# A fused attention and two-layer expert kernel: the first sequence's heads in two parts, and a separate buffer in the weight decode

## The chip, the cores and the metric

The kernel runs on one core of one Trainium2 chip. The metric is the device time of one execution in microseconds (us). Before the change the median of three runs is 915.22 us (913.24 to 915.87). The profiled execution, on which all sums below are made, took 915.09 us.

## What is computed

Three layers follow one another on 2304 tokens (4 sequences of 576, 8 heads of 64, so 512 features). The first is an attention that adds a coarse one over groups of four tokens and a local one over the neighbours less than four tokens away:

```python
q_d = q.reshape(B, H, Sd, factor, D).mean(axis=3)      # the same for k and v; factor = 4, Sd = 144
out_up = np.repeat(sm_attn(q_d, k_d, v_d), factor, axis=2)
mask = np.abs(pos[:, None] - pos[None, :]) < factor
...
attn = np.exp(scores)                                  # scores outside the mask are -1e9
out_local = np.matmul(attn, v)
return out_up + out_local
```

The second is a gated layer, `silu(x @ w_gate) * (x @ w_val) @ w_out`, with 512 x 1536 and 1536 x 512 weights. The third routes each token to one of eight experts (cosine similarity with an embedding) and returns `gate * (relu(x @ w1[e]) @ w2[e])`.

## The kernel before

**The order of the work.** Nothing in this kernel is written in the order in which the engines run it. Every piece of work is a generator; a small planner (`Sched`) keeps a free time for each engine, takes the waiting piece with the lowest priority number that is ready, and emits its instruction. What it costs each operation at stands in the `yield op("ACT", t_act(512))` lines and in the functions `t_dve`, `t_act`, `t_pool`, `t_dma`; buffers are handed out by class (`w`, `ps`, `raw`, ...), and a piece can wait for an event (`yield ("wait", ...)`). The result is one fixed list of instructions for each engine, and each engine then runs its own list strictly in order, so an instruction that waits holds up all behind it.

**Attention.** A pair of heads fills the 128 partitions; there are 16 pairs, four for each sequence. For a pair, `heads` loads q and k (transposed, features on partitions), v for the local part and v for the coarse one into a set of five buffers. `local` cuts the 576 queries into ten units of 58 (64 rows, 64 keys each). In the first sequence it does for a pair: scores on TensorE (L584, 20 small matmuls), the mask added on VectorE while it copies the scores from PSUM (L590, two operations), maximum, subtraction (L594, L596), exponential on ScalarE (L598), sum, reciprocal, product on GpSimd (L606). `local_piece` transposes the weights (L624, 5 transposes of 128 x 128), multiplies with v (L642) and adds the coarse part into the tokens' tile (L649). `down` is the coarse part: sums of four queries and of four keys on VectorE (L498), scores on TensorE (L508, 4 matmuls), exponentials (L524), product (L533), transposes (L541), and the product with v (L558). For the first four pairs (`NV = 4`) v isn't summed over its groups first: TensorE accumulates over the four tokens of a group in 16 matmuls.

**Chunks.** The tokens are then taken in nine chunks of 256 (`CT`). Chunk 0 holds tokens 0 to 255 of the first sequence, chunk 1 tokens 256 to 511, chunk 2 starts with its last 64. `x_split` and `x_piece` split a chunk's 128-feature block k (which is pair k of the sequence) into a rounded part `xhi` (L694, ScalarE) and the rest `xlo` (L697, VectorE for even k, GpSimd for odd); a product then takes three matmuls.

**The gated layer.** `gated` goes over the six 256-wide blocks p of the hidden features, chunks 0 and 1 in turn for each p, and later chunk after chunk. `gemm1` multiplies (L740): for each half j of the block, first all four k of the gate weights, then all four k of the value weights, into one PSUM bank. `act_h` applies the gate, and `gemm2` multiplies with `w_out` (L772). The first `gemm1` needs all four pairs of the first sequence.

**The weights** of this layer come as 64-bit words and are turned into float32 on the chip, in tiles of 128 x 512 (`decode`, 36 of them): VectorE shifts the low words in place (L343), ScalarE scales the high words in place (L346) and then writes a 16-bit number into the upper half of each low word (L350), VectorE joins the two (L353), ScalarE rounds (L358), GpSimd forms the rest (L360). The places that L346 reads and writes lie 8 bytes apart, and so do those that L350 writes.

**Until the first chunk's first block is there**, `keep_warm` fills TensorE's list with matmuls on zeros (L318, 128 x 512, bfloat16): while the event `("x", 0, 0)` isn't set in the plan, one is put wherever the plan has TensorE free. They are fixed entries of the list and run whatever the other engines do.

Of the kernel before, what the change touches and what calls it, by code (L numbers as in the profile page):

```python
# [30 lines left out]
E = 8  # L31
# [22 lines left out]
NCST = P + NPAIR * WK + 3 * E + 4 * NT18 + NOV  # L54
# [151 lines left out]
TOKENS = {'dq': 4, 'raw': 6, 'scatter': 1, 'pat': 4, 'pm': 1, 'early': 4, 'late': 1}  # L206
# [4 lines left out]
NV = 4  # L211
WEIGHT_P = [1.0, 2.0, 3.0, 4.0, 4.5, 4.8]


def build(tc, a):
# [64 lines left out]
    nc.gpsimd.memset(tinit, OOB)  # L280
    nc.scalar.dma_start(out=tab.rearrange("(p n) o -> p (n o)", p=P), in_=tinit)
    def small_consts():
        yield ("lag", 20000)
# [5 lines left out]
        nc.scalar.copy(ones, t01[:, P:2 * P])  # L289
        sc.put("w", t01)  # L290
# [9 lines left out]
    slots("t2", gm, 2, [P, DM])  # L300
# [25 lines left out]
    def decode(cls, src, dst, nm, p, j):  # L326

        yield ("get", "dq")
        raw = yield ("get", cls)
        if j == 1:  # L330
            sc.set((nm, p, "t"))
        r = raw[:, 0:1024].bitcast(I32)
        yield dma(P * 4096)
# [53 lines left out]
    def prep_en():  # L387
        t = yield ("get", "t2")
        t1 = yield ("get", "t2")
        en, junk = t[:E, :], t1[:E, :]  # L390
# [13 lines left out]
        ps = yield ("get", "ps")  # L404
# [6 lines left out]
        sc.put("t2", t)  # L411
        sc.put("t2", t1)
# [28 lines left out]
    def heads(n):  # L441
# [51 lines left out]
    def down(n, sq, sk, sd):  # L493
# [52 lines left out]
        if n < NV:  # L546
            parts = [sd[:GH, 256 * x + D * i:256 * x + D * (i + 1)] for x in range(4) for i in range(4)]
        else:
            parts = [vd_of(sk)[:, x, :] for x in range(4)]
            yield ("wait", ("vfree", n))  # L550
# [9 lines left out]
        if n < NV:  # L560
            sc.set(("vfree", n))
# [7 lines left out]
    def local(n, sq, sk, sv, sa, st):  # L569
# [41 lines left out]
        sc.set(("done", n))  # L611

# [629 lines left out]
    with tc.manual_schedule():  # L1242
# [9 lines left out]
        sc.spawn(6, prep_en(), 0.0)  # L1252
# [64 lines left out]

def consts():
# [55 lines left out]
```

## Time and profile before

| | before |
|---|---|
| three runs, median (lowest to highest) | 915.22 us (913.24 to 915.87) |
| the profiled execution: its time / its span | 915.09 us / 913.3 us |
| TensorE busy, share of the span | 886.4 us, 97% |
| VectorE / ScalarE / GpSimd busy | 443.7 / 395.4 / 287.9 us |
| moved by DMA | 87.99 MB, mean 96 GB/s |

The span runs from the first to the last instruction on the core; 1.8 us of the execution lie outside it. A busy share says only that an instruction was under way: a matmul on zeros counts as one on data, and one at half clock counts double. So the busy share of TensorE is read together with what it was busy with, and with the clock that it was granted.

### The profile page before, as it was taken

The page shows a single profiled execution, that of the slowest core. Times are in us where ns is not written, and L with a number is a line of the kernel's source. Part 1 is how long each engine was busy: PE and PEld are TensorE (multiplying, and loading weights), DVE is VectorE, ACT ScalarE, POOL GpSimd, SP SyncE. Part 2 cuts the span into 40 slices and gives each one's busy share as a digit, 9 for nine tenths or more (in the row PEclk, how much of TensorE's full clock was granted, in tenths as well). Part 3 has the DMA queues.
Part 4 walks back from the last instruction along what each step waited for, and adds up shares of the span by engine and source line. Part 5 has one row for each costly group of instructions (what it writes and reads, how often), then busy time and mean ns, then how long its engine had stood idle before and what let it go on. Part 6 is the DMA issues. An engine that isn't in the chain of part 4 may idle for free. (4 is left out here: it accounts for less than half of the span.)

```text
span 913.3 us, 17270 instructions
## 1 busy us (share of the span) xinstructions
PE 886.4 (97%) x6928; PEld 785.4 (86%) x6934; DVE 443.7 (49%) x1028; ACT 395.4 (43%) x867; POOL 287.9 (32%) x294
## 2 busy tenths in 40 slices
PE   8989999999999999999999999989899999999995
PEld 4679889998989899999999999989788888888884
DVE  4888787644544454445241222356455545544310
ACT  1766989844334333342231322336344444444221
POOL 1456655533423334234122122221310321330211
PEclk9967999999999999999999999999999999999997
DMA  9562364220222022101000000346266554554100
GB/s 275 175 197 91 125 200 162 82 65 13 66 66 65 3 66 67 54 25 55 2 24 1 24 1 1 93 156 191 56 188 192 189 152 160 177 177 129 36 26 27
DMA packets 52484, 87.99 MB, mean 96 GB/s; under 512 B 7790, under 2 KB 24302, under 8 KB 52400
## 3 DMA queue, kind: packets, MB, share of 16 engines
q1 hardware_dynamic: 47664, 76.72, 27.0%
q0 software_dynamic: 4160, 9.48, 3.1%
q8 instruction: 55, 0.90, 0.4%
q10 hardware_dynamic: 576, 0.66, 0.2%
q14 instruction: 29, 0.24, 0.1%
HBM read 77.84 MB, written 10.57 MB: 97 GB/s over the span
## 5 line engine op out<-in xcount | busy, mean ns | idle before, releaser
L740 PE MATMUL ps<-xhi,w 128*128 128x256 f32 x1536 | 305.1, 289 | 2.1 <-ACT aw L524 1.2
L740 PEld LDWEIGHTS ps<-xhi,w 128*128 128x128 f32 x1536 | 248.8, 192 | 7.6 <-issue 2.5
L740 PE MATMUL ps<-xlo,w 128*128 128x256 f32 x768 | 217.9, 284 | 0.7 <-DVE xlo L697 0.7
L740 PEld LDWEIGHTS ps<-xlo,w 128*128 128x128 f32 x768 | 147.8, 192 | 2.3 <-DVE xlo L697 0.9
L710 DVE SCALAR_TENSOR_TENSOR th<-th,ps 128x256 f32<-128x256 f32 x108 | 45.2, 419 | 172.1 <-ACT th L708 172.0
L1066 PE MATMUL ps<-xh,w 128*128 128x336 f32 (+1 forms) x512 | 121.9, 313 | 0.0
L772 PE MATMUL x<-w,hh 128*128 128x512 f32 x384 | 120.9, 396 | 0.0
L718 POOL TENSOR_TENSOR hl<-th,hh 128x256 fp32r<-128x256 f32 x90 | 69.2, 769 | 162.9 <-ACT hh L715 129.6
L708 ACT ACTIVATE th<-ps 128x256 f32<-128x256 f32 x108 | 41.8, 387 | 149.0 <-PE ps L740 145.5
L1066 PEld LDWEIGHTS ps<-xh,w 128*128 128x128 f32 x512 | 88.0, 188 | 2.1
L965 DVE TENSOR_TENSOR w<-w,w 128x1024 fp32r<-128x1024 f32 x64 | 77.6, 1224 | 16.4 <-ACT w L963 15.6
L1091 POOL DMA_INDIRECT out<-t,tb x23 | 24.2, 1054 | 181.5 <-ACT t L1083 169.0
L1076 PE MATMUL x<-w,eh 128*128 128x512 f32 x256 | 81.0, 397 | 0.0
L1052 DVE SCALAR_TENSOR_TENSOR el<-ps,eh 128x336 fp32r<-128x336 f32 (+1 forms) x64 | 31.4, 491 | 100.9 <-ACT eh L1050 100.8
L1066 PE MATMUL ps<-xl,w 128*128 128x336 f32 (+1 forms) x256 | 79.8, 312 | 0.0
L772 PEld LDWEIGHTS x<-w,hh 128*128 128x128 f32 x384 | 68.4, 189 | 12.5 <-issue 1.0
L1050 ACT ACTIVATE eh<-ps 128x336 fp32r<-128x336 f32 (+1 forms) x64 | 28.4, 444 | 108.3 <-PE ps L1066 108.0
L772 PE MATMUL x<-w,hl 128*128 128x512 f32 x192 | 75.0, 390 | 0.0
L715 ACT CAST hh<-th 128x256 fp32r<-128x256 f32 x108 | 44.3, 410 | 65.1 <-DVE th L712 64.8
L963 ACT CAST w<-w 128x1024 fp32r<-128x1024 f32 x64 | 66.1, 1045 | 0.0
L1076 PEld LDWEIGHTS x<-w,eh 128*128 128x128 f32 x256 | 46.5, 188 | 9.2
L360 POOL TENSOR_TENSOR w<-w,w 128x512 fp32r<-128x512 f32 x30 | 41.2, 1382 | 29.4 <-ACT w L358 24.6
(201 smaller groups left out, 1452.4 us busy)
## 6 DMA issues: line engine op xcount, KB each, us to landing
w<-w SPq DMA_DIRECT2D x64, 512.0 KB
w<-w_gate SPq DMA_DIRECT2D x10, 512.0 KB
w<-w_val SPq DMA_DIRECT2D x10, 512.0 KB
w<-w_out SPq DMA_DIRECT2D x10, 512.0 KB
w<-qk SPq DMA_DIRECT2D x16, 291.0 KB
aw<-qk SPq DMA_DIRECT2D x16, 291.0 KB
x2d<-t SPq DMA_DIRECT2D x18, 256.0 KB
w<-vw SPq DMA_DIRECT2D x8, 320.0 KB
```

What stands on the lines that cost most here:

```text
L360: nc.gpsimd.tensor_tensor(out=los, in0=lw.bitcast(F32), in1=his, op=ALU.subtract)
L708: nc.scalar.activation(th, ps[:, 0:CT], AF.Tanh, scale=0.5)
L710: nc.vector.scalar_tensor_tensor(out=th, in0=th, scalar=1.0, in1=ps[:, 0:CT], op0=ALU.add, op1=ALU.mult)
L715: nc.scalar.copy(hh[:, j].bitcast(F32R), th)
L718: e.tensor_tensor(out=hl[:, j].bitcast(F32R), in0=th, in1=hh[:, j].bitcast(F32R), op=ALU.subtract)
L740: nc.tensor.matmul(ps[:, o:o + CT], ww[:, k, fs], xx[:, k, :], start=(k == 0 and n == 0), stop=(k == KD - 1 and n == 2))
L772: nc.tensor.matmul(x2p[c, m], l[:, j, ms], r[:, js], start=(p == 0 and j == 0 and n == 0), stop=(p == NFB - 1 and j == 1 and n == 2))
L963: nc.scalar.copy(hi.bitcast(F32R), raw)
L965: nc.vector.tensor_tensor(out=lo.bitcast(F32R), in0=raw, in1=hi.bitcast(F32R), op=ALU.subtract)
L1052: nc.vector.scalar_tensor_tensor(out=hl[:, j, 0:n].bitcast(F32R), in0=ps[:, 0:n], scalar=0.0, in1=hh[:, j, 0:n].bitcast(F32R), op0=ALU.max ...
L1066: nc.tensor.matmul(ps[:, 0:n], ww[:, k, fs], xx[:, k, 0:n], start=(k == 0 and t == 0), stop=(k == KD - 1 and t == 2))
L1076: nc.tensor.matmul(yt[:m], l, r, start=(first and n == 0), stop=(last and n == 2))
```

## The change

It rewrites the start of the program. The diff below is cut; in the file after the change every later line has a number some 10 to 200 higher, so both numbers are given where they are needed.

- The four pairs of the first sequence (`n < NV`) no longer go through `local` and `down`, but through `local_e`, `down_e` and `piece_e`, each in two parts. Part 0 holds the local units 0 to 4 and the first 64 groups of four queries, enough for tokens 0 to 255; part 1 holds the rest and has a priority number higher by 0.5 (`REST_P`).
- The mask is added by TensorE: a bfloat16 matmul of an identity with a mask of 320 columns (L707) opens the PSUM group, and the scores (L713) accumulate on it. Maximum and subtraction read PSUM (L716, L718); VectorE's two additions of the mask go.
- In the coarse part TensorE sums the queries: the four query tokens of a group are four accumulating matmuls (L655, their stationary operand takes every fourth column of q, 16 bytes apart), for 64 groups at a time. The keys are summed on GpSimd (L634, L636), and so are the values (`down_v`, L507, L509). VectorE's two sums for each of these pairs (L498) go. The local weights are transposed unit by unit as matmuls (L737).
- `xlo` of chunks 0 and 1 is formed on GpSimd for all k (L866).
- `gemm1` of the first chunk and block takes k in the outer loop and holds two PSUM banks from the start (L910), so each pair is used when it comes.
- `decode` writes the shifted low words and the 16-bit numbers into a tile of its own (`sg`, L355, L363), in which those 16-bit numbers lie 4 bytes apart, not 8; the joined word (L366) goes to the old place. The two `sg` tiles become the `t2` tiles of the routing when the last two weight tiles have been decoded.
- Smaller ones: the weights of the embedding (`prep_en`) are prepared in the tile of the triangle constant, earlier; the constants are 96 columns narrower, and a mask tile of 164 KB is loaded behind them on ScalarE's queue (L284); five raw tiles are under way instead of six; the planner counts a DMA at 310 instead of 230 bytes/ns; the set of the fourth pair is given to the weights when it is done.

```diff
-TOKENS = {'dq': 4, 'raw': 6, 'scatter': 1, 'pat': 4, 'pm': 1, 'early': 4, 'late': 1}
+TOKENS = {'dq': 4, 'raw': 5, 'scatter': 1, 'pat': 4, 'pm': 1, 'early': 4, 'late': 1}
...
+        s = yield ("get", "sg")
+        sw = kp(s.bitcast(I32))
         t0 = sc.cur.t
         yield op("DVE", t_dve2(512))
-        nc.vector.tensor_scalar(out=lw, in0=lw, scalar1=29, scalar2=None, op0=ALU.logical_shift_right)
+        nc.vector.tensor_scalar(out=sw, in0=lw, scalar1=29, scalar2=None, op0=ALU.logical_shift_right)
...
-        yield op("ACT", t_act(512))
-        nc.scalar.activation(raw[:, 0:1024].bitcast(F16).rearrange("p (k f t) -> p k f t", k=2, t=4)[:, :, :, 1],
+        yield op("ACT", 790)
+        nc.scalar.activation(s.bitcast(F16).rearrange("p (k f t) -> p k f t", k=2, t=2)[:, :, :, 1],
                              hw.bitcast(F32), AF.Copy, scale=2.0 ** 62)
         yield op("DVE", t_bits(512))
-        nc.vector.scalar_tensor_tensor(out=lw, in0=hw, scalar=3, in1=lw,
+        nc.vector.scalar_tensor_tensor(out=lw, in0=hw, scalar=3, in1=sw,
                                        op0=ALU.logical_shift_left, op1=ALU.bitwise_or)
+        last = left[0] <= 2
+        left[0] -= 1
+        sc.put("t2" if last else "sg", s)
...
-        if n >= NV:
+        if n < NV:
+            sc.spawn(pr, local_e(n, 0, sq, sk, sv, sa))
+            sc.spawn(pr, down_e(n, 0, sq, sk, sd, sa))
             sc.spawn(pr, down_v(n, sk, sd))
-        sc.spawn(pr, local(n, sq, sk, sv, sa, sd))
-        sc.spawn(pr, down(n, sq, sk, sd))
+            sc.spawn(pr + REST_P, local_e(n, 1, sq, sk, sv, sa))
+            sc.spawn(pr + REST_P, down_e(n, 1, sq, sk, sd, sa))
+        else:
+            sc.spawn(pr, down_v(n, sk, sd))
+            sc.spawn(pr, local(n, sq, sk, sv, sa, sd))
+            sc.spawn(pr, down(n, sq, sk, sd))
         yield ("wait", ("done", n))
         early.discard(n)
-        if cls == "we" and len(early) < n_early[0]:
+        if cls == "we" and (len(early) < n_early[0] or NSET <= n < NV):
...
+    def down_e(n, part, sq, sk, sd, sa):
...
+            nc.gpsimd.tensor_tensor(out=k2, in0=k4[:, :, 0:2], in1=k4[:, :, 2:4], op=ALU.add)
...
+        for x, t in enumerate(ts):
+            for i in range(4):
+                for h2 in range(2):
+                    r = slice(h2 * D, (h2 + 1) * D)
+                    nc.tensor.matmul(sp[r, x * G:(x + 1) * G], q4[r, t:t + 64, i], kd[r, :], start=(i == 0), stop=(i == 3))
...
+            nc.scalar.activation(ex[:, x, :], sx[:, x, :], AF.Exp, bias=st[:, 1, x:x + 1], scale=1.0 / 128, accum_out=st[:, 2, x:x + 1])
...
+    def local_e(n, part, sq, sk, sv, sa):
...
+        nc.tensor.matmul(sp[:, 0:k], identb, umask[:, part * k:(part + 1) * k], start=True, stop=False)
+        yield op("PE", 92 * UH)
+        for u in us:
+            t0 = unit0(u)
+            for h2 in range(2):
+                r = slice(h2 * D, (h2 + 1) * D)
+                nc.tensor.matmul(sp[r, c(u)], sq[r, t0:t0 + 64], sk[r, t0:t0 + WK], start=False, stop=(u == us[-1]))
+        s3 = sp[:, 0:k].rearrange("p (u w) -> p u w", w=WK)
+        yield op("DVE", t_dve(k))
+        nc.vector.tensor_reduce(out=mx, in_=s3, axis=AX.X, op=ALU.max)
+        yield op("DVE", t_dve(k) + 60)
+        nc.vector.tensor_tensor(out=A3, in0=s3, in1=mx.unsqueeze(2).to_broadcast([P, UH, WK]), op=ALU.subtract)
+        pput(sp)
...
+                nc.tensor.matmul(tp[r, c(u)], A[r, c(u)], ident[r, r], start=True, stop=True)
...
+    def piece_e(n, i, sq, sv, sa):
...
+        for part in range(2 if i else 1):
+            yield ("wait", ("up", n, part))
+        for c in range((b * S + t0) // CT, (b * S + t1 - 1) // CT + 1):
+            yield ("wait", ("x32", c))
...
-        e, eng, t = (nc.vector, "DVE", t_dve) if k % 2 == 0 else (nc.gpsimd, "POOL", t_pool)
+        e, eng, t = (nc.vector, "DVE", t_dve) if k % 2 == 0 and c > 1 else (nc.gpsimd, "POOL", t_pool)
...
+        if (c, p) == (0, 0):
+
+            pj = []
+            for j in range(2):
+                pj.append((yield ("get", "ps")))
+            for k in range(KD):
+                for j in range(2):
+                    for o, w, nm in ((0, wg, "w_gate"), (CT, wv, "w_val")):
+                        for kk in range(2):
+                            yield ("wait", (nm, p, kk))
+                        wh, wl = (x.rearrange("p (k f) -> p k f", k=KD)[:, k, j * P:(j + 1) * P] for x in w[p])
+                        yield ("wait", ("x", c, k))
+                        yield op("PE", 3 * 120)
+                        xh, xl = (x[:, k, :] for x in xsp[c])
+                        for n, (ww, xx) in enumerate(((wh, xh), (wh, xl), (wl, xh))):
+                            nc.tensor.matmul(pj[j][:, o:o + CT], ww, xx, start=(k == 0 and n == 0 and o == 0),
+                                             stop=(k == KD - 1 and n == 2 and o > 0))
+            for j in range(2):
+                sc.spawn(0, act_h(c, p, pj[j], j))
...
-        sc.spawn(6, prep_en(), 0.0)
+        sc.spawn(3, prep_en(), 0.0)
```

Where the instructions stand is shown at two places. The first is TensorE's list where chunk 0's `gemm1` gets going. Before, in the stretch that ends with the unbroken row of `gemm1` (w_1_135 and w_1_137 are pair 3's v and weights, w_2_529 and w_2_533 pair 4's, `xhi` and `xlo` chunk 0, w_1_143 to w_1_146 the gate and value weights of block 0):

```order
L642 MATMUL ps_1_104<-w_1_135 64x58 x8
L642 MATMUL ps_1_106<-w_1_137,w_1_135 64x58 x8
L508 MATMUL ps_1_107<-w_2_529 72x144 x2
L642 MATMUL ps_1_103<-w_1_135 64x58 x2
L642 MATMUL ps_1_103<-w_1_135 64x54 x2
L584 MATMUL ps_1_105<-w_2_767,w_2_766 64x64 x10
L624 MATMUL ps_1_104<-cn,w_2_533 128x128 x2
L740 MATMUL ps_1_102<-xhi,w_1_143 128x256
L740 MATMUL ps_1_102<-xlo,w_1_143 128x256
L740 MATMUL ps_1_102<-xhi,w_1_144 128x256
L740 MATMUL ps_1_102<-xhi,w_1_145 128x256
```

and after the change, at the first and at the unbroken row (w_1_132 and w_1_134 are pair 2's v and weights; w_1_130 and w_1_135 are q of pairs 2 and 3; w_1_127 and w_1_129 pair 1's v and weights):

```order
L765 MATMUL ps_1_107<-w_1_127 64x58 x8
L765 MATMUL ps_1_107<-w_1_127 64x24 x2
L910 MATMUL ps_1_105<-xhi,w_1_145 128x256
L910 MATMUL ps_1_105<-xlo,w_1_145 128x256
L910 MATMUL ps_1_105<-xhi,w_1_146 128x256
L690 MATMUL ps_1_108<-w_1_123,w_1_121 64x80 x4
L765 MATMUL ps_1_109<-w_1_132 64x58 x8
```

```order
L655 MATMUL ps_1_109<-w_1_130 64x144 x16
L655 MATMUL ps_1_107<-w_1_135 64x144 x16
L765 MATMUL ps_1_108<-w_1_127 64x34 x2
L765 MATMUL ps_1_108<-w_1_129,w_1_127 64x58 x8
L765 MATMUL ps_1_108<-w_1_129,w_1_127 64x54 x2
L910 MATMUL ps_1_105<-xhi,w_1_147 128x256
L910 MATMUL ps_1_105<-xlo,w_1_147 128x256
L910 MATMUL ps_1_105<-xhi,w_1_148 128x256
L910 MATMUL ps_1_106<-xhi,w_1_145 128x256
```

Before, the three products of pair 3's last two pieces (L642) stood in front of the unbroken row, and by then all 576 tokens of all four pairs had been through. Now the first products of `gemm1` stand among the parts 0, and the unbroken row stands behind part 1's scores of pairs 2 and 3 (L655); the rest of part 1 of these two pairs stands behind it.

The second place is GpSimd's list around chunk 0's `xlo`. Before (w_1_143 to w_1_146 as above):

```order
L360 TENSOR_TENSOR w_1_144<-w_1_140,w_1_143 128x512
L533 TENSOR_TENSOR w_1_128<-w_1_128,w_1_129 72x576
L360 TENSOR_TENSOR w_1_146<-w_1_141,w_1_145 128x512
L360 TENSOR_TENSOR w_1_146<-w_1_142,w_1_145 128x512
L697 TENSOR_TENSOR xlo<-x_1_112,xhi 128x256
L697 TENSOR_TENSOR aw_1_117<-x_1_113,aw_1_116 128x256
```

and after the change (w_1_121 to w_1_139 are the pairs' buffers, x_1_114 chunk 0's tokens, x_1_115 chunk 1's):

```order
L509 TENSOR_TENSOR w_1_136<-w_1_138 72x256
L673 TENSOR_TENSOR w_1_123<-w_1_123,w_1_121 128x288
L866 TENSOR_TENSOR xlo<-x_1_114,xhi 128x256
L730 TENSOR_TENSOR w_1_129<-w_1_129 128x320
L730 TENSOR_TENSOR w_1_139<-w_1_139 128x320
L730 TENSOR_TENSOR w_1_134<-w_1_134 128x320
L673 TENSOR_TENSOR w_1_138<-w_1_138,w_1_136 128x144
L376 TENSOR_TENSOR w_1_146<-w_1_141,w_1_145 128x512
L376 TENSOR_TENSOR w_1_146<-w_1_142,w_1_145 128x512
L673 TENSOR_TENSOR w_1_128<-w_1_128,w_1_126 128x288
L866 TENSOR_TENSOR xlo<-x_1_114,xhi 128x256
L376 TENSOR_TENSOR w_1_148<-w_1_143,w_1_147 128x512
```

GpSimd now forms all four `xlo` of chunk 0, between the products of the pairs' second parts and the weights of block 0.

## Rows read from the trace of the kernel before

**Rows 1.** Windows: length; busy PE, PEld, DVE, ACT, POOL (instructions); clock, DMA share, GB/s.
```profile
45.00:50.00 5.00, 3.02 (x60) 2.30 (x60) 4.77 (x11) 4.35 (x10) 2.33 (x2) 1.00 0.91 269
50.00:55.00 5.00, 4.07 (x48) 3.66 (x48) 2.64 (x7) 4.73 (x9) 3.06 (x4) 0.59 0.84 249
70.00:80.00 10.00, 10.00 (x112) 9.10 (x110) 6.96 (x18) 6.46 (x18) 6.08 (x6) 0.59 0.41 137
400.00:600.00 200.00, 200.00 (x1550) 187.94 (x1549) 67.32 (x226) 61.90 (x165) 52.18 (x64) 1.00 0.09 30
```

**Rows 2.** TensorE's timeline: start, duration, line, operation, count [idle before, releaser].
```profile
2.06 10.55 PE L318 MATMUL x<-w 128*128 128x512 bf16 x38 [2.06 <-POOL w L315]
...
17.70 0.71 PE L508 MATMUL ps<-w 64*72 64x144 f32 x8
...
19.31 3.83 PE L318 MATMUL x<-w 128*128 128x512 bf16 x17 [0.16 <-issue]
22.98 0.71 PE L624 MATMUL ps<-cn,w 128*128 128x128 f32 x5
...
32.20 2.18 PE L558 MATMUL ps<-w,w 72*64 72x144 f32 x32
...
36.09 0.68 PE L642 MATMUL ps<-w 64*64 64x58 f32 x16
36.59 0.63 PE L642 MATMUL ps<-w,w 64*64 64x58 f32 x16
...
76.31 0.56 PE L740 MATMUL ps<-xhi,w 128*128 128x256 f32 x1
...
80.44 0.80 PE L584 MATMUL ps<-w,w 64*64 64x64 f32 x20
81.17 0.39 PE L740 MATMUL ps<-xhi,w 128*128 128x256 f32 x1
...
85.35 2.00 PE L740 MATMUL ps<-aw,w 128*128 128x256 f32 x15
```

**Rows 3.** TensorE's groups, 0 to 76.3 us: count, busy us, mean ns, idle before.
```profile
L318 PE MATMUL x<-w 128*128 128x512 bf16 x114 | 28.6, 402 | 2.7 <-POOL w L315 2.1 <-issue 0.6
L584 PE MATMUL ps<-w,w 64*64 64x64 f32 x260 | 9.4, 244 | 0.0
L508 PE MATMUL ps<-w 64*72 64x144 f32 x40 | 5.3, 329 | 1.0 <-DVE w L498 1.0
L624 PE MATMUL ps<-cn,w 128*128 128x128 f32 x22 | 4.5, 316 | 0.0
L740 PE MATMUL ps<-xhi,w 128*128 128x256 f32 x6 | 2.2, 381 | 0.0
L740 PE MATMUL ps<-xlo,w 128*128 128x256 f32 x3 | 1.1, 361 | 0.7 <-DVE xlo L697 0.7
```

**Rows 4.** Timelines of ScalarE, GpSimd and VectorE: single instructions.
```profile
59.22 0.40 ACT L694 CAST xhi<-x 128x256 fp32r<-128x256 f32 x1 [1.51 <-DVE x L649]
...
59.83 2.29 DVE L697 TENSOR_TENSOR xlo<-x,xhi 128x256 fp32r<-128x256 f32 x1
...
19.98 1.25 POOL L606 TENSOR_TENSOR w<-w 128x640 f32<-128x640 f32 x1 [17.98 <-DVE w L604]
...
59.43 1.14 POOL L533 TENSOR_TENSOR w<-w,w 72x576 f32<-72x576 f32 x1 [1.01 <-PE ps L642]
60.54 1.29 POOL L360 TENSOR_TENSOR w<-w,w 128x512 fp32r<-128x512 f32 x1
...
63.33 0.79 POOL L490 TENSOR_TENSOR w<-w 72x256 f32<-72x256 f32 x1
```

**Rows 5.** Groups of the whole span, shapes apart.
```profile
L350 ACT ACTIVATE w<-w 128x512 f16<-128x512 f32 x30 | 40.9, 1379 | 2.5 <-DVE w L602 1.2 <-DVE w L343 0.7 <-DVE enT L409 0.4
L346 ACT ACTIVATE w<-w 128x512 f32<-128x512 f32 x30 | 20.6, 702 | 0.0
L508 PEld LDWEIGHTS ps<-w 64*72 64x72 f32 x64 | 6.1, 149 | 3.0 <-DVE w L498 1.1 <-issue 0.6 <-DVE w L600 0.4
```

More of the change, by code (lines that the diff above doesn't have):

```diff
@@ L278, in build @@
         sc.slots["we"].append(sc.slots["w"].pop(0))
+    um = atp.tile([P, NU * WK // 2], F32, name="um")
+    nc.scalar.dma_start(out=um, in_=a["mask"])
+    umask = um.bitcast(BF16)
     tinit = sc.slots["w"][-1][1].tile()[:, 0:E * EST * 4 // P].bitcast(I32)
@@ L289, in small_consts @@
         nc.scalar.copy(ones, t01[:, P:2 * P])
+        yield ("wait", "en")
         sc.put("w", t01)
@@ L299, in build @@
     slots("th", gm, 2, [P, CT])
[L300 removed]
+    slots("sg", gm, 2, [P, DM])
+    left = [6 * NFB]
     slots("x32", atp, NX, [P, KD, CT], True)
@@ L410, in prep_en @@
         sc.put("ps", ps)
-        sc.put("t2", t)
-        sc.put("t2", t1)
+        sc.set("en")
     def pget(n=1):
@@ L545, in down @@
             pput(tp)
[L546 to L550, printed above, removed]
+        parts = [vd_of(sk)[:, x, :] for x in range(4)]
+        yield ("wait", ("vfree", n))
         k = len(parts) // 4
@@ new lines, in local_e @@
+    def local_e(n, part, sq, sk, sv, sa):
+        us = range(part * UH, (part + 1) * UH)
+        k = UH * WK
+        c = lambda u: slice((u - us[0]) * WK, (u - us[0] + 1) * WK)
+        A = sa[:, part * k:(part + 1) * k]
+        A3 = A.rearrange("p (u w) -> p u w", w=WK)
+        mx = sa[:, 640 + part * UH:640 + (part + 1) * UH]
+        [sp] = yield from pget()
+        yield op("PE", 140)
+        nc.tensor.matmul(sp[:, 0:k], identb, umask[:, part * k:(part + 1) * k], start=True, stop=False)
+        yield op("PE", 92 * UH)
+        for u in us:
+            t0 = unit0(u)
+            for h2 in range(2):
+                r = slice(h2 * D, (h2 + 1) * D)
[5 more added lines that the diff above has]
+        nc.vector.tensor_tensor(out=A3, in0=s3, in1=mx.unsqueeze(2).to_broadcast([P, UH, WK]), op=ALU.subtract)
+        pput(sp)
+        yield op("ACT", t_act(k))
+        nc.scalar.activation(A, A, AF.Exp, scale=1.0 / 8)
+        s1 = sa[:, 650 + part * UH:650 + (part + 1) * UH]
+        yield op("DVE", t_dve(k))
+        nc.vector.tensor_reduce(out=s1, in_=A3, axis=AX.X, op=ALU.add)
+        yield op("DVE", 300)
+        nc.vector.tensor_scalar(out=s1, in0=s1, scalar1=1e-9, scalar2=None, op0=ALU.add)
+        yield op("DVE", 170)
+        nc.vector.reciprocal(s1, s1)
+        yield op("POOL", t_pool(k))
+        nc.gpsimd.tensor_tensor(out=A3, in0=A3, in1=s1.unsqueeze(2).to_broadcast([P, UH, WK]), op=ALU.mult)
+        [tp] = yield from pget()
+        yield ("lag", SLACK)
+        yield op("PE", UH * 107)
+        for u in us:
+            for h2 in range(2):
+                r = slice(h2 * D, (h2 + 1) * D)
+                nc.tensor.matmul(tp[r, c(u)], A[r, c(u)], ident[r, r], start=True, stop=True)
+        yield op("ACT", t_act(k))
+        nc.scalar.copy((sv[:, 640:640 + k], sa[:, 680:680 + k])[part], tp[:, 0:k])
+        pput(tp)
+        sc.spawn(sc.cur.prio, piece_e(n, part, sq, sv, sa))
+        if part == 0:
+            for i in range(2):
+                yield ("wait", ("piece", n, i))
+            sc.set(("done", n))
@@ new lines, in piece_e @@
+    def piece_e(n, i, sq, sv, sa):
+        b, hp = divmod(n, HP)
+        t0, t1 = ((0, CT), (CT, S))[i]
+        tr = lambda u: sv[:, 640 + u * WK:640 + (u + 1) * WK] if u < UH else sa[:, 680 + (u - UH) * WK:680 + (u - UH + 1) * WK]
+        for part in range(2 if i else 1):
+            yield ("wait", ("up", n, part))
+        for c in range((b * S + t0) // CT, (b * S + t1 - 1) // CT + 1):
+            yield ("wait", ("x32", c))
+        [xp] = yield from pget()
+        yield ("lag", SLACK)
+        us = [(u, max(t0, UQ * u), min(t1, UQ * (u + 1))) for u in range(NU)]
+        us = [(u, a, e) for u, a, e in us if a < e]
+        yield op("PE", 2 * len(us) * 60)
+        for u, a, e in us:
+            q0 = -unit0(u)
+            for h2 in range(2):
+                r = slice(h2 * D, (h2 + 1) * D)
+                nc.tensor.matmul(xp[r, a - t0:e - t0], sv[r, u * D:(u + 1) * D], tr(u)[r, q0 + a:q0 + e], start=True, stop=True)
+        up = sq[:, SP6 + 2 * G:SP6 + 3 * G]
+        p0 = t0
+        while t0 < t1:
+            c, o = divmod(b * S + t0, CT)
+            e = min(t1, t0 + CT - o)
+            yield op("DVE", t_dve(e - t0) + 60, -1.0 if i == 0 else None)
+            nc.vector.tensor_tensor(out=x32[c][:, hp, o:o + e - t0].rearrange("p (g f) -> p g f", f=4),
+                                    in0=xp[:, t0 - p0:e - p0].rearrange("p (g f) -> p g f", f=4),
+                                    in1=up[:, t0 // 4:e // 4].unsqueeze(2).to_broadcast([P, (e - t0) // 4, 4]), op=ALU.add)
+            x_left[c, hp] -= e - t0
+            if x_left[c, hp] == 0:
+                sc.set(("xr", c, hp))
+            t0 = e
+        pput(xp)
+        sc.set(("piece", n, i))
```

85 lines of the change are left out of this document (73 added, 12 removed).

## The prediction

> **What bounds the kernel now.** I read the windows first [rows 1]. From 400 to 600 us TensorE is busy for 200 of 200 us at full clock, so what stands behind the start goes as fast as TensorE can, and a microsecond won or lost at the start arrives at the end. In the windows between 45 and 80 us this isn't so: TensorE is busy for 3.02 of 5 us from 45 to 50, and after that its granted clock falls to 0.59 of full, on average, in two windows that look well filled. Busy at half clock (1.2 of 2.4 GHz) is half lost.
>
> Then TensorE's timeline and its groups [rows 2, 3]: 38 matmuls on zeros end at 12.6 us, 114 run in all, and the gated layer's unbroken row begins at 76.3 us (81.17 and 85.35 are later pieces of it). By then only 9 of its matmuls had run. What it waits for shows in single instructions [rows 4]: ScalarE's rounding of a block of the tokens at 59.22 us, which VectorE's addition released. All 576 tokens of a pair go through VectorE and ScalarE before the pair's block is there, and the first `gemm1` needs all four. So the bound at the start is the chain of the four pairs, not TensorE.
>
> **The change, part by part.** All sums are against the profiled execution, 915.09 us (913.3 us of span, 1.8 around it); the median, 915.22, is 0.1 above it. The three runs lie within 2.6 us of each other, so a difference of up to 0.3%, 2.7 us, is one that a measurement can't tell from none.
>
> *When does the unbroken row begin after the change?* TensorE's new list is known, so I add it up, at full clock and without a wait. Prices per record, where a float32 matmul on small tiles is two records, and a transpose or a matmul of the gated layer one: a matmul on zeros 0.216 (17 between 19.31 and 22.98), its 320-column sister for the mask 0.135 by columns; L655 0.068, from L558 with as many columns (32 in 2.18; the 8 of L508, 0.71 with their tail, say 0.089 at most, 4 us more on all 192); L713 and L737 0.73 for 20 records, from the second sequence's scores, which use one row half and one column half of the array as these do (80.44 to 81.17); L680 0.14 (5 in 0.71); L765 0.031 (16 between 36.09 and 36.59); L690 half of L655, 0.034; the gated layer's 0.133 (15 in 2.00) [rows 2].
> - A pair: 2 masks 0.27, 4 x 0.73 = 2.92, 48 records of L655 3.26, 6 transposes 0.84, 16 records of L690 0.54, 44 of L765 1.37. Sum 9.2 us.
> - Four pairs 36.8. Behind the unbroken row's start stand, by the list, part 1's L680 and L690 of pairs 2 and 3 (1.1 and 0.6), L765 of the same (1.5) and pair 3's L737 (0.7), 3.9 together: 32.9 before it, and 0.4 for the first three matmuls of L910.
> - Matmuls on zeros: 31 stand ahead of the first mask, so that starts 7 x 0.216 ahead of 12.6, at 11.1 us; 48 more, 10.4 us, stand between. The mask tile is third on its queue, where before a larger table stood.
> - 11.1 + 10.4 + 32.9 + 0.4 = **54.8 us**, against 76.3: 21.5 us earlier.
>
> *What is done at that point?* After: the four pairs less 3.9, plus 0.4. Before, at 76.3: the four pairs, and beside them 100 records of the second sequence's L584 (260 less 160) at 0.0365, 8 of its L508 (40 less 32) at 0.089, 2 transposes and 9 of L740 [rows 2, 3]: 3.7 + 0.7 + 0.3 + 1.2 = 5.9. So the change is 3.5 + 5.9 = 9.4 us behind in work. What TensorE's matmuls for the masks and query sums add is in these numbers already. A mean of 0.59 from 70 to 80 us is half clock until about 78 [rows 1], so the old row lost another 1 us there. Gain without a wait: 21.5 - 9.4 + 1 = **13.1 us**.
>
> *GpSimd* gets the sums of keys and values, `xlo` and the split products. From its first sum of keys to chunk 0's fourth `xlo` its list has 38 operations: 8 of 512 columns at 1.29, 9 of 256 at 0.79, 13 of 288 or 320, between 0.79 and the 1.14 of 576 (I take 0.9), and 8 of 144, below 0.79 (I take 0.5): 10.3 + 7.1 + 11.7 + 4.0 = 33 us [rows 4]. The first six, 5.7 us, need loads only. The rest starts when the first softmax has its sums: before, the product came at 19.98, 7.4 us behind the first scores, so now at about 18.5, and 18.5 + 27.3 = 46 us. The fourth `xlo` is wanted near 54.8 + 36 x 0.133 = 59.6, so GpSimd has 13 us of cover at the end, but next to none at the products in between, for which TensorE's list waits.
>
> *VectorE* loses eight sums of 576 columns, eight additions of the mask and the four `xlo` of even k, and *ScalarE's* 16-bit write should shorten from 1.38 us towards the 0.70 us that a 4-byte write at the same step takes [rows 5]. I take 0.8, with the ends 0.70 and 1.38. None of it is priced in the sum: both have to finish ahead of TensorE's list, and the write is worth 0.6 x 5 = 3 us of ScalarE at most before the row begins. Earlier preparation of the embedding, narrower constants, five raw tiles and the fourth set's early release I cost at nothing: they lie beside TensorE's 11 us of zeros or behind the row's start; if the weights of the second block come late because of them, TensorE's next wait is there.
>
> *What the waits cost.* VectorE's operations are held up beside GpSimd's: the `xlo` at 59.83 took 2.29 us and ended only with GpSimd's two, at 59.43 and 60.54 (their last end 61.83) [rows 4]. GpSimd is now busy nearly all the time from 18 to 46 us, and VectorE holds a dozen shifts, joins and small scalings there. The Trainium skill, SBUF — State Buffer, "Who interferes with whom", says that a VectorE instruction with two SBUF inputs, or in a two-port mode, and a GpSimd instruction that reads SBUF shut each other out for the whole instruction; the trace agrees, with those 2.29 us. It speaks against moving work to GpSimd. Such holds reach TensorE only where the list has no zeros left, from about 35 us on. Ends: nothing, if the cover holds; 13.1 us and the gain is gone, if TensorE falls to half clock as it did at 50. I take **4 us**, nearer the low end because the list is full where the old one had empty stretches.
>
> 915.1 - 13.1 + 4 = **906.0 us**.
>
> **The rivals.**
> - *The cover holds.* No wait reaches TensorE, and the small matmuls cost a little less than taken (L713 and L737 at the 0.031 of L642, which uses the array in the same way: 16 x 20 x 0.0055 = 1.8 us): 915.1 - 13.1 - 1.8 = 900. For: the 48 zeros between give every other engine 10 us. Against: the old list, with as many zeros in front, fell into waits at 45. Chance 0.18.
> - *Held-up VectorE, starved TensorE, half clock.* The list waits on the products, the clock falls as in the 50 to 55 window, and the gain is eaten: about 915. For: 3.02 busy of 5 us came before the fall at 50 [rows 1]. Against: 13 us of cover at the end. Chance 0.13.
> - *Slower: the queries' stationary loads.* L655 loads every fourth column, 16 bytes apart; no load of the trace does that. A contiguous load of this size takes 0.149 us [rows 5] and hides behind the 0.068 us of a record. If it no longer hides, each of the 192 records costs 0.149 - 0.068 = 0.081 more: 15.6 us on a list that has no room, 906.0 + 15.6 = 921.6. The point is 9.1 / 192 = 0.047 us per record. For: they stand in TensorE's list ahead of the unbroken row. Against: half that step costs ScalarE nothing that shows, 512 columns in 0.70 us [rows 5]. Chance 0.13. The Trainium skill, SBUF — State Buffer, "Door 1: The DMA port swizzle", says that SBUF is read in lines of 16 bytes and each access to a new line pays; by it every element of these loads would. No row of this trace shows it for TensorE.
> - *The separate tile changes nothing*, the 16-bit write stays at 1.38: 3 us of ScalarE more before the row, 909. Chance 0.04.
>
> **How the numbers follow.** Forecast 0.52 (its own range 901 to 911), cover 0.18, half clock 0.13, slower loads 0.13, write unchanged 0.04. Faster by more than 0.3%: 0.52 + 0.18 + 0.04 and a little of the half-clock case, 0.76. Slower: the loads and a little of the half-clock case, 0.15. Same 0.09. The range takes in the cover case with 3 us below it for prices that hold tails, the half-clock case, and loads that hide in part: 897 to 920.
>
> **What would show it.** Right: the unbroken row of L910 begins near 55 to 59 us, fewer than 80 matmuls on zeros, the clock at full in every window from 20 us on, L655's 16 records in about 1.1 us, the write L363 near 0.8 us. Wrong: L655 above 1.8 us for 16 records (slow loads); windows below 0.8 of the clock between 40 and 70 (starved); TensorE idle behind 60 us, waiting for weights that ScalarE or GpSimd decode late; or a gain at 60 us that is missing at the end, which would say that the later stretches aren't TensorE's.

## The result, and the profile after

The changed kernel takes 907.05 us (median, 906.03 to 907.56), beside 915.55 (913.24 to 917.74) for the kernel before: ratio 0.9901, 95% interval 0.9879 to 0.9923. That is 0.8 to 1.2% faster. The profiled execution has a span of 905.8 us (before 913.3) and takes 907.56.

The same windows as in [rows 1], of the changed kernel, with two more behind 200 us and the stretch from 13 to 60 us:

```profile
45.00:50.00 5.00, 5.00 (x128) 4.45 (x127) 1.86 (x6) 4.93 (x14) 3.30 (x4) 1.00 0.01 3
50.00:55.00 5.00, 4.34 (x83) 3.95 (x79) 4.74 (x9) 4.01 (x11) 4.52 (x4) 1.00 0.62 205
70.00:80.00 10.00, 9.25 (x99) 7.99 (x96) 10.00 (x29) 6.95 (x21) 6.52 (x8) 1.00 0.69 207
200.00:205.00 5.00, 3.51 (x18) 3.42 (x19) 3.97 (x19) 2.85 (x12) 1.99 (x2) 0.68 0.00 0
205.00:210.00 5.00, 3.55 (x31) 3.32 (x30) 2.83 (x12) 1.83 (x6) 3.06 (x3) 0.98 0.01 0
13.00:60.00 47.00, 45.36 (x727) 35.84 (x728) 28.88 (x80) 29.98 (x94) 30.42 (x41) 1.00 0.60 197
```

The two stretches that ran at half clock before, from 50 and from 70 us, are at full clock, and TensorE is busy in nearly all of them. What is left is a hole at 200 us: 1.5 us idle in each of two windows, and a mean clock of 0.68 in the first. The kernel before waited in this part too, 1.2 and 0.9 us at 213 and 218 us, but at full clock.

TensorE's timeline (as [rows 2]), then groups of instructions (as [rows 3, 5]; shapes apart), then the last `xlo` of chunk 0 on GpSimd (as [rows 4]):

```profile
2.06 9.39 PE L328 MATMUL x<-w 128*128 128x512 bf16 x31 [2.06 <-POOL w L325]
11.28 0.30 PE L707 MATMUL ps<-um,cn 128*128 128x320 bf16 x1
11.51 0.80 PE L713 MATMUL ps<-w,w 64*64 64x64 f32 x20
12.24 0.31 PE L707 MATMUL ps<-um,cn 128*128 128x320 bf16 x1
...
15.69 1.26 PE L655 MATMUL ps<-w 64*64 64x144 f32 x16
...
20.01 2.24 PE L655 MATMUL ps<-w 64*64 64x144 f32 x32
...
50.87 0.30 PE L707 MATMUL ps<-um,cn 128*128 128x320 bf16 x1 [0.66 <-DVE x L772]
...
57.07 0.39 PE L910 MATMUL ps<-xhi,w 128*128 128x256 f32 x1
...
201.92 0.58 PE L929 MATMUL ps<-xhi,w 128*128 128x256 f32 x1 [1.49 <-DVE th L881]
...
208.59 0.38 PE L929 MATMUL ps<-xhi,w 128*128 128x256 f32 x1 [1.45 <-DVE th L881]
```
```profile
L328 PEld LDWEIGHTS <-w 128*128 128x128 bf16 x76 | 7.5, 106 | 11.0 <-issue 3.3 <-POOL w L325 1.7
...
L655 PEld LDWEIGHTS ps<-w 64*64 64x64 f32 x192 | 12.2, 191 | 1.6 <-issue 1.5
...
L363 ACT ACTIVATE sg<-w 128x512 f16<-128x512 f32 x30 | 23.4, 792 | 0.1
```
```profile
52.73 0.91 POOL L866 TENSOR_TENSOR xlo<-x,xhi 128x256 fp32r<-128x256 f32 x1
```

The unbroken row of the gated layer (L910) begins at 57.07 us, where it began at 76.31. 76 matmuls on zeros ran (their loads are counted, since some matmul records are missing); before, 119 of these loads.

**Where the gain is on its way.** The activation behind the gated layer (L708 before, L877 after) runs once per half block in the same order in both, so it tells how far one kernel is ahead, as long as ScalarE runs it as soon as its product is there. The 19th, the 25th and the 103rd of it, before and then after; ahead of them, TensorE's 48 matmuls that form the 19th and the 20th product:

```profile
173.80 5.86 PE L740 MATMUL ps<-aw,w 128*128 128x256 f32 x48
...
181.11 0.47 ACT L708 ACTIVATE th<-ps 128x256 f32<-128x256 f32 x1
...
206.36 0.38 ACT L708 ACTIVATE th<-ps 128x256 f32<-128x256 f32 x1 [3.43 <-PE ps L740]
...
601.23 0.38 ACT L708 ACTIVATE th<-ps 128x256 f32<-128x256 f32 x1 [2.94 <-PE ps L740]
```
```profile
164.95 5.86 PE L929 MATMUL ps<-aw,w 128*128 128x256 f32 x48
...
168.19 0.37 ACT L877 ACTIVATE th<-ps 128x256 f32<-128x256 f32 x1
...
199.68 0.38 ACT L877 ACTIVATE th<-ps 128x256 f32<-128x256 f32 x1 [1.28 <-PE ps L929]
...
595.65 0.38 ACT L877 ACTIVATE th<-ps 128x256 f32<-128x256 f32 x1 [2.92 <-PE ps L929]
```

The lead is 12.9 us at the 19th, 6.7 at the 25th, 5.6 at the 103rd, and 7.5 at the end of the span. The 19th misleads, though. Half of the 48 matmuls, 2.85 us, is its product; ScalarE came to it 4.4 us after that before, with weight decoding ahead of it in its list, and 0.4 us after it in the changed kernel. TensorE's own lead at this place is 173.80 - 164.95 = 8.9 us. So the start gave 8.9 us, of which 5.6 are left at the 103rd and 7.5 at the end; the first fall comes at 200 us.

### The profile page after: what moved, and what is told of

It is laid out like the page before. It is cut to its first block, busy times and chain, and to the rows that moved or that the text cites. A ratio compares the mean times of both kernels' runs of the same rounds, so it can differ in the third digit from the quotient of the medians.

```text
span 905.8 us, 17729 instructions
## 1 busy us (share of the span) xinstructions
PE 882.6 (97%) x7137; PEld 785.2 (87%) x7143; DVE 433.8 (48%) x1016; ACT 377.7 (42%) x879; POOL 300.0 (33%) x322
## 5 line engine op out<-in xcount | busy, mean ns | idle before, releaser
L929 PE MATMUL ps<-xhi,w 128*128 128x256 f32 x1504 | 298.8, 289 | 2.9 <-DVE th L881 2.9
L929 PEld LDWEIGHTS ps<-xhi,w 128*128 128x128 f32 x1504 | 243.2, 192 | 8.7 <-DVE th L881 3.3
L929 PE MATMUL ps<-xlo,w 128*128 128x256 f32 x752 | 213.1, 283 | 0.0
L929 PEld LDWEIGHTS ps<-xlo,w 128*128 128x128 f32 x752 | 144.5, 192 | 1.3
L887 POOL TENSOR_TENSOR hl<-th,hh 128x256 fp32r<-128x256 f32 x90 | 71.8, 797 | 171.3 <-ACT hh L884 138.3
L877 ACT ACTIVATE th<-ps 128x256 f32<-128x256 f32 x108 | 41.1, 382 | 164.1 <-PE ps L929 159.5
L1280 POOL DMA_INDIRECT out<-sg,tb x23 | 24.5, 1066 | 184.9 <-ACT sg L1272 171.0
L1265 PE MATMUL x<-w,el 128*128 128x512 f32 x128 | 50.4, 394 | 0.0
```

The lines of the kernel that those rows point to most:

```text
L877: nc.scalar.activation(th, ps[:, 0:CT], AF.Tanh, scale=0.5)
L887: e.tensor_tensor(out=hl[:, j].bitcast(F32R), in0=th, in1=hh[:, j].bitcast(F32R), op=ALU.subtract)
L929: nc.tensor.matmul(ps[:, o:o + CT], ww[:, k, fs], xx[:, k, :], start=(k == 0 and n == 0), stop=(k == KD - 1 and n == 2))
L1265: nc.tensor.matmul(yt[:m], l, r, start=(first and n == 0), stop=(last and n == 2))
```

## The experiments

The runs are told by question, not in the order in which they ran. One table holds their readings: the median, the ratio to the kernel before (on the same chip), and, from the windows 13 to 60 and 60 to 110 us of each profile, how long TensorE was idle and what the clock took, as length times (1 - granted clock). The last column counts loads of zeros.

| kernel | us | ratio, 95% interval | idle 13-110 | clock 13-110 | zeros |
|---|---|---|---|---|---|
| before | 915.5 to 917.3 | 1 | 5.8 | 12.2 | 119 |
| the change | 907.05 | 0.9901 (0.9879-0.9923) | 2.5 | 0 | 76 |
| e1 own buffer alone | 918.17 | 1.0018 (0.9998-1.0038) | 3.1 | 15.8 | 119 |
| e2 more zeros alone | 909.49 | 0.9928 (0.9900-0.9956) | 2.4 | 3.5 | 169 |
| e6 both of these | 910.63 | 0.9938 (0.9921-0.9955) | 0 | 0 | 174 |
| e3 change, decode in place | 915.50 | 0.9991 (0.9973-1.0008) | 4.7 | 5.0 | 77 |
| e5 same, planner told 1380 ns | 915.25 | 0.9993 (0.9976-1.0010) | 6.0 | 3.5 | 76 |
| e4 change, heads whole first | 923.20 | 1.0065 (1.0042-1.0088) | 2.0 | 3.5 | 109 |
| e10 change, one priority | 912.37 | 0.9965 (0.9950-0.9979) | 3.7 | 7.0 | 73 |
| e8 change, old loops | 916.00 | 0.9990 (0.9973-1.0007) | 6.8 | 8.5 | 64 |
| e11 change, two xlo on VectorE | 912.40 | 0.9970 (0.9958-0.9983) | 4.2 | 3.5 | 74 |
| e7 change, adjacent queries | 907.25 | 0.9897 (0.9883-0.9912) | 1.6 | 0 | 76 |
| e9 change, fewer banks for heads | 928.44 | 1.0146 (1.0128-1.0163) | 3.4 | 0 | 76 |
| e12 change, third heads later | 901.90 | 0.9846 (0.9824-0.9868) | 1.7 | 0 | 76 |

The theory that they test: the change wins because TensorE's list reaches the unbroken row early and never runs dry on the way, so that the clock holds. Its rivals: that the clock alone, or one part alone, made the gain.

**e1, the kernel before with the buffer of its own.**

```diff
-    slots("t2", gm, 2, [P, DM])
+    slots("sg", gm, 2, [P, DM])
-        nc.vector.tensor_scalar(out=lw, in0=lw, scalar1=29, ...)
+        nc.vector.tensor_scalar(out=sw, in0=lw, scalar1=29, ...)
```


> The kernel before, and of the change only the buffer of its own for the low words of the gated weights (the heads stay whole). Theory (the gain comes from the earlier unbroken row of the gated layer): the row still begins at 74 to 77 us, since the pairs are late as before; the 16-bit write takes 0.79 us instead of 1.38, which is off the path; time 913 to 916, within 0.3% of before. Rival (the decode is what held the start): ScalarE wins 0.6 us on each of the decodes ahead of the row, some 3 us in all, and the time falls to 910 to 912.

No gain: 1.0018. The clock took 15.8 us up to 110 us, more than before. The buffer alone doesn't move the start.

**e2, the kernel before with zeros until the fourth block.**

```diff
-        while ("x", 0, 0) not in sc.ev:
+        while ("x", 0, 3) not in sc.ev:
```


> The kernel before, with its matmuls on zeros kept up until the fourth block of the tokens is there (50 more of them). Theory: the granted clock is 1.00 from 20 us to the row's start, but the row still waits for the pairs and begins at 72 to 77 us; only the part of TensorE's own work that ran at half clock between 50 and 78 us comes back: time 910 to 915. Rival (the clock alone made the gain): the time falls to 906 to 909, as with the whole change. A third: the zeros stand in the way of work that is ready, 50 x 0.216 = 10.8 us, and the time is up to 920.

1 - 0.9928 = 0.0072, 6.6 us of 916.55: most of what the whole change gives, by nothing but TensorE kept busy. The median, 909.49, lies in the gap between what the theory (910 to 915) and the rival (906 to 909) had asked for, so the rival has the larger part of the truth: in the kernel before, the half clock between 50 and 78 us was the larger cost, not the wait for the pairs. Four runs took 908.7 to 909.6 at a mean clock of 0.994 to 0.996, two 913.6 and 913.9 at 0.990. The profiled one is of the latter, and shows one wait that no zero covers, behind which the clock fell to half. That this wait is what the faster four lack is likely, but they have no profile.

```profile
61.74 0.58 PE L740 MATMUL ps<-xlo,w 128*128 128x256 f32 x1 [1.95 <-DVE xlo L697]
...
60.00:110.00 50.00, 47.84 (x497) 38.07 (x498) 43.14 (x91) 33.48 (x82) 31.08 (x29) 0.93 0.44 138
```

**e6, e1 and e2 together** (both of these edits).

> The kernel before with both the zeros kept up until the fourth block of the tokens and the buffer of its own (the first two experiments together). The zeros alone gave 909.5, the buffer alone 918. Theory (the buffer pays only where TensorE doesn't run at half clock and the decode is the next thing late): 904 to 908, as good as the whole change or better. Rival (the order of the pairs is what lets the decode's time count): the buffer adds nothing, 909 to 913.

```profile
13.00:60.00 47.00, 47.00 (x569) 29.45 (x568) 41.43 (x88) 29.10 (x82) 22.42 (x18) 1.00 0.75 228
60.00:110.00 50.00, 50.00 (x549) 40.43 (x547) 44.40 (x96) 34.43 (x91) 33.14 (x30) 1.00 0.45 146
```

From 13 to 110 us TensorE is never idle and always at full clock, and still the time is 910.63: the theory's 904 to 908 fell, the buffer added nothing that can be measured. 98 matmuls on zeros more than in the whole change are 98 x 0.216 = 21 us of TensorE. Zeros hold the clock, but don't bring the tokens earlier. That is what the order of the pairs has to do; what it gives beyond the zeros is small here, 0.9938 - 0.9901 = 0.0037 or 3.4 us, and the ends of the two intervals touch.

**e3 and e5, the whole change with the low words decoded in place.**

```diff
-        s = yield ("get", "sg")
-        nc.vector.tensor_scalar(out=sw, in0=lw, ...)
+        nc.vector.tensor_scalar(out=lw, in0=lw, ...)
-        yield op("ACT", 790)
+        yield op("ACT", 1080)
```
(1380 in e5.)

> The whole change without the buffer of its own: low words decoded in place, the 16-bit write at a step of 8 bytes. Theory: that write takes 1.38 us again; some 4 to 5 decodes lie ahead of the row, 0.6 us each, and the list gives ScalarE cover: row at 57 to 60 us, time 907 to 910. Rival: the buffer is what makes the earlier row possible at all, the clock breaks, and the time goes back above 912.

> The whole change with the low words decoded in place, as in the third experiment, but with the planner told 1380 ns for the 16-bit write, what it takes, instead of 1080. Theory (the write's own 0.58 us on ScalarE, 15 times between 20 and 110 us, is what cost the gain): still 913 to 917. Rival (the order was laid out for a write that is shorter than it is): the lists fit again and the time is 907 to 910.

Without the buffer all of the gain is gone: 0.9991 - 0.9901 = 0.009, 8.2 us. What the planner is told doesn't matter (e5). Of the decode's operations the write is the one that is longer in place; VectorE's shift is even shorter there (549 ns, L353, against 731 for L355 in the change). In e3 the first activation behind the gated layer comes at 67.67 us, as early as in the change (68.29). Then the decode falls behind. In the longest of TensorE's waits the embedding's transposes (L416) wait for VectorE's scaling (L413), which stood behind shifts and joins that wait for the write (L361):

```profile
L361 ACT ACTIVATE w<-w 128x512 f16<-128x512 f32 x30 | 41.2, 1372 | 0.1
...
L353 DVE TENSOR_SCALAR w<-w 128x512 int32<-128x512 int32 x30 | 16.4, 549 | 2.3 <-DMA w<-w_gate 1.4 <-DMA w<-w_out 0.8
...
103.15 0.41 PE L416 MATMUL ps<-cn,w 8*128 8x8 f32 x4 [1.54 <-DVE w L413]
...
60.00:110.00 50.00, 46.48 (x490) 39.10 (x487) 43.82 (x86) 36.78 (x82) 37.94 (x34) 0.90 0.50 158
```

**e4, the first piece waits for both parts again.**

```diff
-        for part in range(2 if i else 1):
+        for part in range(2):
```


> The whole change, but the first piece of a head waits for both parts of its coarse attention, so chunk 0's tokens no longer come first; masks and sums of queries stay on TensorE. The list has 33 more matmuls on zeros and all of part 1's small matmuls ahead of the row. Theory (the row's start sets the gain): 33 x 0.216 = 7.1 us later for the zeros, and the work ahead of the row is only moved: row at 66 to 72 us, time 912 to 916. Rival (what pays is the work taken off VectorE and GpSimd, not the order): the time stays at 907 to 909.

The theory's side, and dearer than it said: 1.0065 - 0.9901 = 0.0164, 15 us. The first activation comes at 83 us, 15 us later. 33 more zeros (7.1 us) and two waits of 0.9 and 1.0 us at 72 and 74 us, with the clock at 0.50 from 75 to 80, are part of it; how the rest divides the run doesn't tell.

**e10, both parts at one priority.**

```diff
-REST_P = 0.5
+REST_P = 0.0
```


> The whole change with both parts of the first heads at one priority (the second part was 0.5 behind). The list has 3 fewer matmuls on zeros. Theory (part 0 ahead of part 1 is what brings chunk 0's tokens early, and the list is full only in that order): more of part 1 stands ahead of the row, up to 3.9 us of TensorE, and one or two breaks of the clock come between 55 and 110 us: 909 to 916. Rival (the dependence alone, with chunk 0's piece waiting for part 0 only, does it): 906 to 908.

```profile
65.00:70.00 5.00, 3.81 (x77) 3.05 (x76) 4.86 (x10) 4.50 (x12) 4.03 (x5) 0.99 0.62 209
70.00:75.00 5.00, 5.00 (x42) 4.34 (x39) 5.00 (x9) 1.12 (x3) 4.92 (x5) 0.50 0.02 7
```

As the theory had it: 5.9 us lost. The pattern is the one of the kernel before: a window with 1.2 us of idle time, and the next ones at half clock.

**e8, the gated layer's first block in the old order of loops.**

```diff
-        if (c, p) == (0, 0):
+        if False:
```


> The whole change, but the first block of the gated layer in the old order of loops, one bank after the other over all four blocks of the tokens. Theory (the new order only lets the first matmuls go before the fourth block is there; its zeros are 12 fewer, 2.6 us): within 2 us of the whole change, 906 to 910. Rival (without it TensorE waits for the third and fourth xlo with nothing in its list, and the clock falls): above 911.

The rival: 8.1 us lost, the whole gain. I had taken this part for a nicety. Without it TensorE has nothing to do between the pairs' last steps:

```profile
55.00:65.00 10.00, 6.83 (x88) 5.69 (x86) 9.31 (x15) 5.79 (x15) 9.02 (x9) 0.80 1.03 276
90.00:105.00 15.00, 12.29 (x73) 10.21 (x74) 13.33 (x28) 12.69 (x32) 10.15 (x8) 0.77 0.57 188
```

**e11, two `xlo` of chunks 0 and 1 back on VectorE.**

```diff
-        ... if k % 2 == 0 and c > 1 else ...
+        ... if k % 2 == 0 else ...
```


> The whole change with the xlo of even k in chunks 0 and 1 back on VectorE, as before. Theory (VectorE is held up beside GpSimd just where chunk 0's tokens come together): two xlo of chunk 0 take 1 to 2.3 us instead of 0.8, the row begins 1 to 3 us later, and a break of the clock is likely: 909 to 915. Rival (GpSimd and VectorE both have cover there): 906 to 908.

The time is the theory's (6.3 us lost), its mechanism isn't: chunk 0's two `xlo` took 0.41 and 0.43 us on VectorE, at 38.33 and 48.71 us, when GpSimd was idle, so they don't test whether it holds VectorE up; the first activation came at 68.37. What came instead is a wait of 1.5 us at L527 for VectorE's L881 behind the row's start, and a clock of 0.93 from 60 to 110 us. VectorE isn't later there: the same wait ends at 70.92 us, and in the change at 71.08. TensorE comes to it 1 us earlier; in the change it waited there for 0.4 us.

**e7, sums over adjacent queries.**

```diff
-  q4[r, t:t + 64, i], kd[r, :]
+  sq[r, i * 128 + t:i * 128 + t + 64], kd[r, :]
```


> The whole change, with the sums of queries taken from adjacent columns instead of every fourth one (so other queries are summed; the instructions are the same in number and size, and so is their order). Theory (the stationary loads at a step of 16 bytes hide beside the matmuls): L655 stays at 1.2 to 1.3 us for 16 records, time within 0.3% of the whole change, 905 to 910. Rival (the step makes the loads longer, and they set L655's pace): 16 records take 1.0 us or less, and the time falls by 192 x 0.01 to 0.02 us or more, 902 to 905.

No difference that can be measured. The loads themselves are shorter, 132 ns where the strided ones take 191, or 11 us over all 192, and the matmuls hide nearly all of it: 1.20 us for 16 records, and 1.26 with the stride.

```profile
L655 PEld LDWEIGHTS ps<-w 64*64 64x64 f32 x192 | 11.5, 132 | 1.6 <-issue 1.5
...
15.35 1.20 PE L655 MATMUL ps<-w 64*64 64x144 f32 x16
```

**e9 and e12, the hole at 200 us.** There TensorE's list has the gated layer use one PSUM bank, one of the buffers that TensorE writes its products to, for four halves in a row: of the six, the heads of the third sequence hold two, chunk 1's second layer two, and the routing of chunk 0 one. The waits end with L881, the last reader of the bank.

```diff
-        for _ in range(2):
+        for _ in range(3):
             yield ("get", "pat")
-    head_sets = lambda n: [(0,), (1,)] if n // HP == 1 else [(0, 1)]
+    head_sets = lambda n: [(0,), (1,)] if n // HP in (1, 2) else [(0, 1)]
```


> The whole change, and beside it the heads of the third sequence in the small sets that the second's have, and three tokens of PSUM banks, not two, kept from the heads while chunk 1's second layer holds two banks. In the whole change four halves of the gated layer in a row (96 matmuls) use one and the same bank at 200 us; here no two neighbours do. Theory (those two waits of 1.5 us and the 3.4 us at half clock behind the first are the bank's): TensorE's idle time from 195 to 260 us falls from 2.9 us to under 1, and the time by 3 to 4.6 us, to 902 to 904. Rival (the heads that get fewer banks become late instead): the wait only moves, 906 to 909.

e9 took the bank from the heads all the time from chunk 1's tokens on: the hole at 200 us is gone (0.25 us idle from 195 to 260), but TensorE is idle for 10.2 of 85 us from 110 to 195, and the time is 1.0146. Both the theory's 902 to 904 and the rival's 906 to 909 fell; which of its two edits opens the new waits the run doesn't tell.

```diff
+        yield ("wait", ("lg", 1, 0) if b == 2 else ("x32", 0))
         pr = sc.cur.prio
```


> The whole change, and the heads of the third sequence start (behind their loads) only when chunk 1's second layer has given back its first bank; before that place nothing differs. In the whole change four halves of the gated layer in a row (96 matmuls) use one bank at 200 us; here no two neighbours do until later ones at 250 us. Theory (the two waits of 1.5 us at 202 and 208 us and the 3.4 us at half clock are the bank's, and third heads have 50 us of cover): idle from 195 to 260 us falls from 2.9 us to under 1, no half clock there, time 902 to 904. Rival (the third heads are late for chunk 4, at 265 us, or other waits come in their place): 906 to 912.

e12 only lets the third sequence's heads start later, behind their loads. Windows 195 to 260 us, first of the kernel before (with its two waits), then of the change, then of e12:

```profile
213.76 0.39 PE L740 MATMUL ps<-xhi,w 128*128 128x256 f32 x1 [1.22 <-ACT aw L524]
...
218.34 0.39 PE L740 MATMUL ps<-xhi,w 128*128 128x256 f32 x1 [0.90 <-DVE th L712]
...
195.00:260.00 65.00, 62.88 (x565) 57.14 (x565) 28.72 (x104) 23.51 (x71) 22.69 (x26) 1.00 0.14 46
```
```profile
195.00:260.00 65.00, 62.07 (x624) 56.93 (x623) 29.71 (x106) 21.96 (x67) 22.73 (x26) 0.97 0.17 51
```
```profile
195.00:260.00 65.00, 65.00 (x584) 60.10 (x582) 30.85 (x107) 24.98 (x75) 24.25 (x28) 1.00 0.11 37
```

The 2.9 us of idle time and the 65 x 0.03 = 2 us of the clock are gone. **901.90 us, ratio 0.9846 (0.9824 to 0.9868), the fastest of all**, at the lower edge of the theory's 902 to 904. It also saves the 2.1 us that the kernel before was idle there.

## Why the prediction was right, point by point

The forecast was 906.0 us (897 to 920), the result 907.05: right in sign and size. Not all of its steps were, and that the total is off by 1 us only is in part luck: errors of the steps below cancel.

- **When the row begins.** 54.8 us without a wait, 57.07 measured. The list holds 45 matmuls on zeros behind the first mask, not the 48 that I counted, so the sum should have been 0.6 lower. Of the 2.9 us that are then left, idle time from 13 to 60 us makes 1.6 (47.00 - 45.36), and the masks 0.8: a matmul for the mask takes 0.23 us start to start (11.28 to 11.51), where 0.135 was taken, and eight stand ahead of the row. L655 at 0.068 was right (32 records start to end in 2.2 us), so were L713 (20 records in 0.73 start to start) and the first mask at 11.1 (11.28).
- **The gain without a wait, 13.1 us.** It was smaller. TensorE's lead is 8.9 us at the 19th product; with the 2.5 us that it was idle up to 110 us put back, 11.4.
- **What the waits cost, 4 us.** I had looked for them ahead of the row, on GpSimd and VectorE. They took 2.5 us up to 110 us, without a fall of the clock, so that loss and the gain were both taken too high, and their difference, 9.1, came out as the 8.9 us of lead. The larger loss came at 200 us, where no step of mine looked: a PSUM bank, with the clock that fell behind it, 2.9 + 2 = 4.9 us, where the kernel before lost 2.1. e12 gives the 4.9 back. That its 901.9 is close to 915.1 - 13.1 = 902.0 shows nothing: the lead wasn't 13.1, and e12 saves the 2.1 us as well. The prediction's criterion "clock at full in every window from 20 us on" failed there.
- **GpSimd.** The fourth `xlo` ended at 53.6 us, where 46 was forecast: the list of operations was right, but it is not busy nearly all the time (17.5 of 28 us from 18 to 46). It was still ahead of the place where it is wanted.
- **The separate buffer.** The write took 0.79 us, as taken. Its worth was mis-sized: 3 us in the prediction, counted only ahead of the row (909 without it); 8.2 in e3 (915.5). There the first activation is as early as in the change, and TensorE's idle time from 60 to 110 us is 3.5 us against 0.8, so most of the loss lies behind the row's start. "None of it is priced in the sum: both have to finish ahead of TensorE's list" was the step that failed.
- **The slower rival.** Its condition, loads that no longer hide, didn't come (e7). The Trainium skill, SBUF — State Buffer, "Door 1: The DMA port swizzle", says that each access that crosses to a new line of 16 bytes pays; the trace agrees in the loads' own time (191 against 132 ns), while the kernel's time doesn't change.
- **The half-clock rival (915).** Not what the change does, but what nearly every version of it with one part undone does: e3, e5, e8 at 0.999, e10 and e11 at 0.997. The losses of e3, e4, e8, e10 and e11, 8.2, 15, 8.1, 5.9 and 6.3 us, add up to several times the gain of 9.1, so they aren't shares of it: any one of them opens a hole in TensorE's list between 55 and 110 us, and the clock adds nearly as much again or more (4.7 us idle and 5.0 of clock in e3, 3.7 and 7.0 in e10). Each of these versions is also laid out anew by the planner, so a part's own worth can't be read from them to a microsecond.
- **A ledger of the start.** From the table, before against after: idle time 5.8 - 2.5 = 3.3 us, clock 12.2, zeros 43 x 0.216 = 9.3, together 24.8 us won; the span fell by 7.5. So the rest of TensorE's time grew by 17. By the traces, each record taken from its start to the next one's and half clock counted half, the attention's matmuls make 12.5 us of that (83.0 before, 95.5 after): L655 alone takes 192 x 0.066 = 12.7 us, where the first four pairs' scores of sums before, 32 records of L508 at 0.089, took 2.8. The hole at 200 us makes 2.8 (4.9 - 2.1), and the gated layer's matmuls about 2.7. The change buys an unbroken start with more work on TensorE.

## What to carry to other kernels

Where an engine's clock falls behind an idle stretch, the worth of an edit isn't the time of the instructions that it removes, but whether it closes the last hole in that engine's list; so parts of such a change can't be judged one at a time, and each should be tried undone from the whole as well as alone. After a win at the start, follow one instruction of the limiting engine that both kernels run in the same order through the whole span: the place where its lead shrinks (here 8.9 us up to 190, 5.6 at 600) is the next thing to mend. An instruction of another engine can be late for reasons of its own, as the 19th activation was by 4.4 us. Filling a wait with idle matmuls recovers the clock, but not the wait.

## What was not expected of the hardware

- A ScalarE write of 512 16-bit values takes 1.38 us at a step of 8 bytes (L350 before, L361 in e3) and 0.79 at a step of 4 bytes (L363), while a 4-byte write at a step of 8 bytes takes 0.70 [rows 5].
- Executions of one program can differ by 4.5 us along with their mean clock: e2's runs at 909 us have 0.994 to 0.996, those at 913.7 us 0.990, and 0.005 of 909 us is 4.5.
